# Half-height matmuls for the score tiles and dense blocks, columns loaded tile by tile, and the dots' small chain on GpSimd

## The chip, the cores and the metric

One Trainium2 chip, one of its cores. The metric is the device time of one execution in microseconds (us); before, the median of three runs was 1926.75 us (1924.97 to 1935.35).

Short names used below: PE is TensorE, PEld its weight loads, DVE VectorE, ACT ScalarE, POOL GpSimd, SP the SyncE queue that issues most DMAs.

## The reference

The layer takes x of 2048 tokens by 512 numbers, normalizes it and returns x + attention(xn) + experts(xn).

```
xn = layernorm(x)
# attention: 32 query heads of 16 numbers, one key/value head
scores = einsum("bhqd,bkd->bhqk", q, k) * (16 ** -0.5)
o = softmax(scores) @ v ; attention = o @ wo
# experts: 32 heads, 64 x 64 = 4096 experts addressed by two keys
s1 = einsum("nhd,ed->nhe", q1, k1) ; s2 = einsum("nhd,ed->nhe", q2, k2)
# the two best of each, their four sums, the two best of these: experts and gates
g = softmax(top_s) ; ue = u[top_e] ; ve = v[top_e]
act = gelu(einsum("nd,nhkd->nhk", xf, ue))
experts = einsum("nhk,nhk,nhkd->nd", g, act, ve)
```

## The kernel before

**Stages.** The tokens are four groups of 512 (GT = 4 tiles of 128 tokens). A short start normalizes, transposes x into `XT` (four tiles of 128 by 512 columns, each as a high and a low part) and projects q, k and v. Then 256 attention steps run, and everything else is put into the gaps of these steps.

**One attention step** (`att_steps`) issues on PE, in this order: four score matmuls (`sc`, two pairs; a pair is two matmuls of 64 rows each, one on the upper and one on the lower half of the array), eight `pv` matmuls in tiles of 32 columns, four more `sc`, and then the *fill*: whatever `run_scores` takes from the generator `score_thread`. ACT makes the exponentials (`pt`) of the four pairs. Between the `pv` and the second `sc` the function `mid` records the expert work: the tanh of a group of four gathered experts (`tanhs`), work of earlier steps put off in the lists `ON_ACT`, `LAST`, `LATER` and `BEHIND`, the dots of gathered rows with xn (`dots`), the weighted sums (`adds`), and new gathers. A fill ends when the cost counter `spent` (0.235 for one full matmul, `UNIT`) reaches the step's aim or has grown by 4.0 (`MOST`).

**What fills.** For each of 32 pairs (token group, chunk of heads) in `SEQ`, `item` makes four score tiles `psc`: 12 matmuls of 128 rows by 512 columns, whose result DVE reads with eight MAX8 and eight FIND_INDEX8. After the fourth tile `batch` turns these into gates and indices on DVE and POOL. For token groups 0 and 1 the experts are gathered row by row with indirect DMAs on the POOL queue (512 gathers, 128 groups of four). For groups 2 and 3 `dense` goes through all experts instead: 32 blocks, each with a `pact` tile (12 matmuls, then ACT Square and two DVE reads, later tanh and a split into `wd`), and for each pair of blocks four `pout` tiles (`sums`: six matmuls each and one DVE add). Before the blocks a stage of `pg` matmuls spreads the gates. `block_out` makes the attention's output (`pwo`).

**Buffers.** All of `psc`, `pact`, `pout`, `pwo`, `pg`, `pw` share three PSUM buffers:

```
xtile = lambda name: ps.tile([P, 512], F32, name=name, tag="x", bufs=3)
```

A new tile takes the buffer that was given back first; its first matmul waits for the last reader of the tile that held it.

**Order.** Inside the 256 steps the order on each engine is the order of recording; nothing is rescheduled. Every engine works through its list in order, so a wait holds up all that stands behind it on that engine.

**The dots' chain.** After the fourth dot of a group, three small DVE operations of 128 by 4 (`CHAIN`, L997 to L999) prepare the gelu; ACT does the tanh (L1004) in the next step; a fourth small DVE operation (`weigh`, L1011) makes the weights w of the four sums (L1023).

**Columns.** `load_phase2_xt` loads the next token group's columns into a new set of `XT` tiles (four DMAs of 512 KB) in the last tile of the old group, and `score_thread` ends that fill early.

Of the kernel before, what the change touches and what calls it, by code (L numbers as in the profile page):

```python
# [55 lines left out]
def tile_kernel(ctx, tc, x, wq, wkv, wo, wqT, kT, uv, ub, vb, out):  # L56
# [70 lines left out]
    XT, XN, ACC, XP = {}, {}, {}, [None]  # L127
# [65 lines left out]
    def project_kv(g):  # L193
        p = stile("pkv")[:, 0, :]
        n = 0
        for k in range(KC):
            for a, b in TERMS:
                w = (wkv_h, wkv_l)[a]
                nc.tensor.matmul(p[:32, :], w[:, k, :], XT[g][k][:, b, :], start=n == 0, stop=n == 11)
                n += 1  # L200
# [20 lines left out]
    def project_q(g, wqs):  # L221
        pq = xtile("pqs")
        for r in range(KC):
            p = stile("pq")[:, 0, :]
            n = 0
            for k in range(KC):
                for a, b in TERMS:
                    nc.tensor.matmul(p, wqs[k][:, a, r * P:(r + 1) * P], XT[g][k][:, b, :],
# [282 lines left out]

    def item(n_, ti, make=()):
# [5 lines left out]
        if jb == 0:  # L518
            m8 = small.tile([P, BT, 8, 8], F32, name="m8", bufs=1)
            i8 = small.tile([P, BT, 8, 8], U32, name="i8", bufs=1)  # L520
            M8[ph, c, b], I8[ph, c, b] = m8, i8
        m8, i8 = M8[ph, c, b], I8[ph, c, b]
        p = xtile("psc")

        last = ti == TPH - 1
        more = nc_ is not None and not (ph >= NSP and c == NC - 1)
        read = more and n_ + 1 >= NC
        n = 0
        for k in range(KC):
            for a, bb in TERMS:  # L530
                nc.tensor.matmul(p, XT[g][k][:, a, j * P:(j + 1) * P], WC[n_][k][:, bb, :],  # L531
                                 start=n == 0, stop=n == 11)
                n += 1
            if read and ti == 0 and k < 2:
                wp_read(n_ + 1, range(2 * k, 2 * k + 2))
            if last and more and nph != ph:
                load_phase2_xt(nph, k)
# [5 lines left out]
        for s in range(8):  # L543
            nc.vector.max(m8[:, jb, s, :], p[:, s * E:(s + 1) * E])  # L544
        for s in range(8):
            nc.vector.max_index(i8[:, jb, s, :], m8[:, jb, s, :], p[:, s * E:(s + 1) * E])  # L546
        if jb == BT - 1:
            batch(ph, c, b)
# [107 lines left out]
    def dense(DG, after):  # L656
# [72 lines left out]
        def activations(b, us, p):  # L729
            n = 0  # L730
            for k in range(KC):
                for a, c in TERMS:
                    nc.tensor.matmul(p, us[:, a, k * P:(k + 1) * P], XT[DG][k][:, c, :],  # L733
                                     start=n == 0, stop=n == 11)
                    n += 1
                yield k

        def first(b):
            p = xtile("pact")
            for k in activations(b, early[b], p):  # L740
                if k < KC - 1:
                    yield 3 * UNIT
            g, y = gate_rows(b), hh[:, b, :]
            nc.scalar.activation(y, p, AF.Square, scale=C_CUB ** 0.5)
            nc.scalar.copy(g, p)
            nc.vector.scalar_tensor_tensor(y, y, C_IN, p, op0=OP.add, op1=OP.mult)

            def go():
                nc.scalar.activation(y, y, AF.Tanh)
                behind(lambda: nc.vector.scalar_tensor_tensor(y, y, 1.0, g, op0=OP.add, op1=OP.mult))  # L750

            LATER.append(go)
            yield 3 * UNIT
# [11 lines left out]
        yield from first(0)  # L765
        rest_of_first = first(1)
        yield from islice(rest_of_first, 2)
# [37 lines left out]
        yield from rest_of_first  # L805
# [43 lines left out]
        held, ready, used = [], [], [0]  # L849

        def sums():

            used[0] += 2
            if formed[0] < used[0]:
                flush()
            for j in range(GT):
                p = xtile("pout")
                n = 0
                for wd, vs in ready:
                    for a, c in TERMS:  # L860
                        nc.tensor.matmul(p, wd[0][:, a, j * P:(j + 1) * P], vs[:, c, :], start=n == 0, stop=n == 5)  # L861
                        n += 1
                acc = ACC[GT * DG + j]
                nc.vector.tensor_add(acc, acc, p)  # L864
                yield 6 * UNIT

        stt = nc.vector.scalar_tensor_tensor
        for b in range(NB):
            wd = []
            if b > 1:  # L870
# [5 lines left out]
                p = xtile("pact")  # L876
                for k in activations(b, splits[b][0], p):
                    if k == 0:
                        store(lambda b=b: fetch_gates(b + 1))
                        if b % 2 == 0 and b > 2:  # L880
                            later_split(b + 2)
                        if b == 2:

                            store(load_totals)
                    if k == KC - 1 and b == NB - 1 and after is not None:
                        wp_read(after, range(2))
                    if b == NB - 1 and after is not None:
                        load_phase2_xt(SEQ[after][0], k)
                    if k < KC - 1:
                        yield 3 * UNIT  # L890

                if b not in fetched:
                    if b > 3 and formed[0] < b - 2:
                        flush()
                    run(STORES)
                    assert b in fetched
            vs = splits.pop(b)[1]
            gy = gates[b]
            if b > 2:
                gates.pop(b - 1)  # L900
            g, y = (gy[:, 0, :], gy[:, 1, :]) if b > 1 else (gy[:, b, :], hh[:, b, :])

            def gated(g=g, p=None):
                stt(g, g, 1.0 / GS, p, op0=OP.mult, op1=OP.mult)

            def whole(y=y, g=g):
                stt(y, y, 1.0, g, op0=OP.add, op1=OP.mult)

            def scaled(y=y, g=g):
                multiplied[0] += 1  # L910
                stt(g, g, 1.0 / GS, y, op0=OP.mult, op1=OP.mult)

            def high(y=y if b > 1 else g, wd=wd):
                wd.append(late[0].tile([P, 2, 512], F32R, name="wd", tag="wd", bufs=4))
                nc.scalar.copy(wd[0][:, 0, :], y)
                behind(lambda: low(y, wd[0]))

            def low(y, wd):
                nc.vector.tensor_tensor(out=wd[:, 1, :], in0=y, in1=wd[:, 0, :], op=OP.subtract)  # L919
                formed[0] += 1  # L920

            if b > 1:
                nc.scalar.activation(y, p, AF.Square, scale=C_CUB ** 0.5)
                stt(y, y, C_IN, p, op0=OP.add, op1=OP.mult)
                LAST.append(lambda y=y: nc.scalar.activation(y, y, AF.Tanh))
                if b == 3:

                    behind(lambda gated=gated, g=g, p=p: gated(g, p))
                else:
                    gated(g, p)  # L930
                behind(whole)
                LATER_ACT.append(high)
            else:
                LATER.append(lambda scaled=scaled, high=high: (behind(scaled), on_act(high)))
            held.append((wd, vs))
            if b > 1:
                yield 3 * UNIT
# [4 lines left out]
            for _ in range(b - 1 if b in (2, 3) else 0):  # L942
                if out_ready():
                    block_out()
                    yield 3.6
            if b % 2:
                if b > 1:
                    later_split(b + 2)
# [6 lines left out]
        yield from sums()  # L955
        if after is not None:
            wp_read(after, range(2, KC))
        OUTS.extend(range(GT * DG, GT * DG + GT))
# [8 lines left out]
    CHAIN = []  # L967
# [13 lines left out]
    def dot(m):  # L981
# [8 lines left out]
        if i == SB - 1:  # L990
# [5 lines left out]
            stt = nc.vector.scalar_tensor_tensor  # L996
            CHAIN.append(lambda: stt(q, a, C_CUB, a, op0=OP.mult, op1=OP.mult))  # L997
            CHAIN.append(lambda: stt(y, q, C_IN, a, op0=OP.add, op1=OP.mult))
            CHAIN.append(lambda: nc.vector.tensor_tensor(out=pairs(ga), in0=pairs(a), in1=gg, op=OP.mult))  # L999
            TH[n], GA[n] = y, ga  # L1000

    def tanh(n):
        th = small.tile([P, SB], F32, name="gth", bufs=3)
        nc.scalar.activation(th, TH[n], AF.Tanh)  # L1004
        TH[n] = th

# [365 lines left out]
```

## Time and profile before

| | |
|---|---|
| median of three runs | 1926.75 us |
| the profiled execution | 1925.78 us, its span 1924.1 us |
| PE busy | 1863.8 us (97%) |
| DVE busy | 1634.0 us (85%) |
| ACT busy | 1294.2 us (67%) |
| POOL busy | 700.8 us (36%) |
| `psc`, `pact`, `pout` on PE | 1536, 768 and 768 matmuls |
| DMA | 255 GB/s on average |

Busy time is the union of an engine's instructions. Matmuls overlap each other, so a start-to-start distance tells more than a duration. The span goes from the first to the last instruction; 1.7 us of the execution lie around it.

### The profile page before, as it was taken

The numbers are of one execution on the slowest core, as the hardware profiler recorded it, in microseconds if no ns is written. First come the engines' busy times: TensorE is split into PE (matmuls) and PEld (weight loads), VectorE is DVE, ScalarE is ACT, GpSimd is POOL, SyncE is SP. The second block draws the span as 40 slices with busy tenths as digits, with TensorE's granted clock in tenths as the row PEclk, the third lists the DMA queues.
The fourth block names the chain that finished last, engine by engine and source line by source line (L and its number), as shares of the span: only waits on it lengthen the run. The fifth ranks groups of instructions, "written<-read, shape, count | busy, mean of one in ns | idle before, by whom it ended". The sixth has DMA issues, their size and how long they took to land.

```text
span 1924.1 us, 34929 instructions
## 1 busy us (share of the span) xinstructions
PE 1863.8 (97%) x10990; PEld 991.8 (52%) x10990; DVE 1634.0 (85%) x6381; ACT 1294.2 (67%) x1803; POOL 700.8 (36%) x920
## 2 busy tenths in 40 slices
PE   6979999999999999999999999999999999999998
PEld 3634444555555554555555554555555455555553
DVE  6627787989998977999999897899988779999994
ACT  3346666655557887787877555555578777888873
POOL 1203334434452223343444444355422134344430
PEclk9989999999999899999999999999988899999999
DMA  7857789787773778888999987876736778899882
GB/s 274 315 186 278 266 272 301 279 296 251 249 246 122 233 240 249 253 288 270 287 300 309 362 287 237 280 256 220 242 105 220 249 215 292 271 284 286 282 277 84
DMA packets 234395, 491.13 MB, mean 255 GB/s; under 512 B 93396, under 2 KB 93396, under 8 KB 234204
## 3 DMA queue, kind: packets, MB, share of 16 engines
q0 software_dynamic: 73728, 268.47, 42.0%
q1 hardware_dynamic: 159240, 219.56, 34.9%
q8 instruction: 88, 1.44, 0.3%
q10 hardware_dynamic: 1236, 0.82, 0.1%
q14 instruction: 103, 0.84, 0.1%
HBM read 427.41 MB, written 56.07 MB: 251 GB/s over the span
## 4 chain that ended last, share of the span: by engine, by line
PE 85%; DMA 3%; ACT 3%; DVE 1%; issue 1%; SPq 0%; DVEq 0%; ACTq 0%
PE pv L340 24%; PE psc L531 18%; PE sc L326 17%; PE pact L733 9%; PE pout L861 9%; PE pg L815 3%; PE pwo L433 2%; ACT pt L329 2%; PE pw L486 1%; DMA wqt<-in_wqT_dram 1%; DMA dinv<-rc 1%; DMA wk<-dw 1%; PE pwt L493 0%; PE pwl L408 0%; DMA qa<-dqh 0%
## 5 line engine op out<-in xcount | busy, mean ns | idle before, releaser
L329 ACT ACTIVATE pt<-sc 128x1024 f32<-128x1024 f32 x1024 | 993.7, 1026 | 461.9 <-PE sc L326 460.5
L976 POOL DMA_INDIRECT g<-in_uv_dram,idx x512 | 556.8, 1087 | 1002.0 <-DVE xa L1023 531.0
L340 PE MATMUL pv<-pt,vaug 128*32 128x512 f32 x4096 | 516.4, 623 | 0.0
L531 PE MATMUL psc<-wk,xt 128*128 128x512 f32 x1536 | 388.7, 401 | 4.1 <-DVE wk L496 3.5
L326 PE MATMUL sc<-qa,kaug 64*128 64x512 f32 x2048 | 384.2, 451 | 8.6 <-ACT pt L329 8.4
L1023 DVE SCALAR_TENSOR_TENSOR xa<-g,w,xa 128x512 f32<-128x512 f32 x512 | 371.7, 744 | 0.1
L988 DVE CUSTOM_DVE_ANT_0 g<-g,xa 128x512 f32<-128x512 f32 x512 | 335.5, 681 | 7.4 <-DMA g<-in_uv_dram,idx 7.4
L531 PEld LDWEIGHTS psc<-wk,xt 128*128 128x128 f32 x1536 | 277.9, 188 | 107.7 <-issue 37.5
L326 PEld LDWEIGHTS sc<-qa,kaug 64*128 64x128 f32 x2048 | 155.9, 185 | 329.3 <-ACT pt L329 218.8
L340 PEld LDWEIGHTS pv<-pt,vaug 128*32 128x32 f32 x4096 | 109.6, 111 | 257.0 <-issue 255.4
L546 DVE FIND_INDEX8 i<-m,psc 128x8 uint32<-128x64 f32 x1024 | 206.3, 220 | 0.0
L733 PE MATMUL pact<-xt,wk 128*128 128x512 f32 x768 | 195.9, 400 | 0.0
L861 PE MATMUL pout<-wk,wd 128*128 128x512 f32 x768 | 194.8, 401 | 0.2 <-DVE wd L919 0.2
L544 DVE MAX8 m<-psc 128x8 f32<-128x64 f32 x1024 | 146.2, 213 | 41.1 <-PE psc L531 40.3
L861 PEld LDWEIGHTS pout<-wk,wd 128*128 128x128 f32 x768 | 140.8, 188 | 47.3 <-DVE act L988 5.5
L733 PEld LDWEIGHTS pact<-xt,wk 128*128 128x128 f32 x768 | 139.4, 188 | 48.5 <-issue 17.5
L698 DVE TENSOR_TENSOR wk<-rw,wk 128x512 fp32r<-128x512 f32 x128 | 84.8, 683 | 9.7 <-ACT wk L697 9.7
L864 DVE TENSOR_TENSOR da<-da,pout 128x512 f32<-128x512 f32 x128 | 82.8, 679 | 10.1 <-PE pout L861 10.0
L783 DVE TENSOR_TENSOR oh<-oh 128x2048 f16<-128x2048 f16 x64 | 78.0, 1219 | 0.8 <-ACT oh L759 0.6
L815 PEld LDWEIGHTS <-oh 128*128 128x128 f16 x1024 | 68.4, 162 | 13.8 <-issue 6.4
L1011 DVE SCALAR_TENSOR_TENSOR w<-gth,ga 128x4 f32<-128x4 f32 x128 | 20.4, 159 | 64.5 <-ACT gth L1004 64.0
L815 PE MATMUL pg<-oh 128*128 128x32 f16 x1024 | 73.5, 247 | 0.6 <-DVE oh L786 0.5
(159 smaller groups left out, 1411.1 us busy)
## 6 DMA issues: line engine op xcount, KB each, us to landing
wk<-dw SPq DMA_DIRECT2D x96, 512.0 KB
wqt<-in_wqT_dram SPq DMA_DIRECT2D x32, 512.0 KB
dw<-wk SPq DMA_DIRECT2D x32, 512.0 KB
rw<-in_ub_dram SPq DMA_DIRECT2D x64, 256.0 KB
rw<-in_vb_dram SPq DMA_DIRECT2D x64, 256.0 KB
gy<-dg SPq DMA_DIRECT2D x64, 256.0 KB
qa<-dqh SPq DMA_DIRECT2D x128, 64.0 KB
g<-in_uv_dram,idx POOLq DMA_INDIRECT x512, 6.0
```

What stands on the lines that cost most here:

```text
L326: nc.tensor.matmul(p[:, b, :], kaug[o:o + 64, kc * P:(kc + 1) * P], QA[u][o:o + 64, i, :], start=True, stop=True)
L329: nc.scalar.activation(pt, p, AF.Exp, scale=SCALE)
L340: nc.tensor.matmul(PV[u][32 * j:32 * j + 32, :], vaug[:, kc, :], pt[:, b, :], start=kc == 0, stop=kc == 15)
L531: nc.tensor.matmul(p, XT[g][k][:, a, j * P:(j + 1) * P], WC[n_][k][:, bb, :], start=n == 0, stop=n == 11)
L544: nc.vector.max(m8[:, jb, s, :], p[:, s * E:(s + 1) * E])
L546: nc.vector.max_index(i8[:, jb, s, :], m8[:, jb, s, :], p[:, s * E:(s + 1) * E])
L733: nc.tensor.matmul(p, us[:, a, k * P:(k + 1) * P], XT[DG][k][:, c, :], start=n == 0, stop=n == 11)
L815: nc.tensor.matmul(p[:, i * NB:(i + 1) * NB], oa[:, :, i], ob[:, :, i], start=True, stop=True)
L861: nc.tensor.matmul(p, wd[0][:, a, j * P:(j + 1) * P], vs[:, c, :], start=n == 0, stop=n == 5)
L976: nc.gpsimd.indirect_dma_start(out=gt, out_offset=None, in_=uv, in_offset=bass.IndirectOffsetOnAxis(ap=IDX[ph, c, ti][:, s:s + 1], axis=0))
L988: nc.vector.tensor_tensor_reduce(u, u, XN[TPH * ph + ti], scale=1.0, scalar=0.0, op0=OP.mult, op1=OP.add, accum_out=a[:, i:i + 1])
L1023: nc.vector.scalar_tensor_tensor(acc, v, w[:, i:i + 1], acc, op0=OP.mult, op1=OP.add)
```

## The change

**Half products.** From the last chunk of token group 0 on (`n_ >= NC - 1`), and in the dense blocks, `item`, `first`, `dense` and `sums` no longer issue matmuls; they yield objects `Tile` that hold the 12 or 6 operand pairs and a function `done` for what reads the result. `run_scores` collects the tiles of one fill and hands them to `products`. Of these, the last ones with up to 12 matmuls together are done *half*: each matmul of 128 rows becomes two of 64 rows. The upper halves (rows 0 to 63) are issued in this fill, alternating with the lower halves (rows 64 to 127) of the tiles kept from the fill before (`HALF`), whose `done` follows. Other tiles of the fill are done whole, after that. Where the upper list has 12 and the lower 6 (or the other way round), the six left over are issued alone.

**Columns tile by tile.** There is one set of `XT` tiles. `load_xt` loads 128 of the 512 columns (four DMAs of 128 KB) after the last use of these columns, in `done` of each tile; the early end of the fill is gone.

**Chain on GpSimd.** The chain is recorded at once after the fourth dot as four POOL operations, and the weights are two POOL operations recorded with the tanh; `CHAIN` and `weigh` are gone.

```diff
+    def products(tiles):
+        n, first = 0, []
+        while tiles and not tiles[-1].alone and n + len(tiles[-1].steps) <= 12:
+            n += len(tiles[-1].steps)
+            first.insert(0, tiles.pop())
+        a = [(t, i, 0) for t in first for i in range(len(t.steps))]
+        b = [(t, i, 1) for t in HALF for i in range(len(t.steps))]
+        if first or any(t.alone and t.steps for t in tiles):
+            for i in range(max(len(a), len(b))):
+                for run_ in (a, b):
+                    if i < len(run_):
+                        t, k, half = run_[i]
+                        t.mm(k, half)
+            for t in HALF:
+                t.done(t.p)
+            HALF[:] = first
+        for t in tiles:
+            t.whole()
...
+        def mm(self, i, half=None):
...
+                o = slice(64 * half, 64 * half + 64)
+                nc.tensor.matmul(self.p, w[o], v[o], start=i == 0 and half == 0, stop=i == n - 1 and half == 1)
...
+        tile_ = Tile("psc", steps, done)
+        if n_ >= NC - 1:
+            yield tile_
+            return
...
-            if b % 2:
-                if b > 1:
-                    later_split(b + 2)
-                if ready:
-                    for _ in range(2):
-                        if formed[0] < used[0] + 2:
-                            yield None
-                    yield from sums()
-                ready, held = held, []
+            if b % 2 == 0 and b > 3:
+                yield from ready(b - 4)
+                yield from sums(b - 4, (2, 3))
+            if b % 2 and b > 1:
+                yield from ready(b - 3)
+                yield from sums(b - 3, (0, 1))
...
-            stt = nc.vector.scalar_tensor_tensor
-            CHAIN.append(lambda: stt(q, a, C_CUB, a, op0=OP.mult, op1=OP.mult))
-            CHAIN.append(lambda: stt(y, q, C_IN, a, op0=OP.add, op1=OP.mult))
-            CHAIN.append(lambda: nc.vector.tensor_tensor(out=pairs(ga), in0=pairs(a), in1=gg, op=OP.mult))
+            V = nc.gpsimd
+            V.tensor_mul(q, a, a)
+            V.tensor_scalar(q, q, C_CUB, C_IN, op0=OP.mult, op1=OP.add)
+            V.tensor_mul(y, q, a)
+            V.tensor_tensor(out=pairs(ga), in0=pairs(a), in1=gg, op=OP.mult)
...
     def tanh(n):
         th = small.tile([P, SB], F32, name="gth", bufs=3)
-        nc.scalar.activation(th, TH[n], AF.Tanh)
-        TH[n] = th
+        nc.scalar.activation(th, TH.pop(n), AF.Tanh)
+        ga = GA.pop(n)
+        w = small.tile([P, SB], F32, name="w", bufs=3)
+        nc.gpsimd.tensor_mul(w, th, ga)
+        nc.gpsimd.tensor_add(w, w, ga)
+        WT[n] = w
...
-    def load_phase2_xt(g, k):
-        if k == 0:
-            XT[g] = []
-        xt = big.tile([P, 2, 512], F32R, name="xt", tag="xt", bufs=4)
-        nc.sync.dma_start(raw(xt[:]), d_xt[g - 1][k])
-        XT[g].append(xt)
+    def load_xt(g, j=None):
+        c = slice(0, 512) if j is None else slice(j * P, (j + 1) * P)
+        for k in range(KC):
+            nc.sync.dma_start(raw(XT[k][:, :, c]), d_xt[g - 1][k][:, :, c])
```

More of the change, by code (lines that the diff above doesn't have):

```diff
@@ L510, in tile_kernel, with __init__, whole @@
     BT = 4
+    class Tile:
+        def __init__(self, name, steps, done, alone=False):
+            self.name, self.steps, self.done, self.alone, self.p = name, steps, done, alone, None
+        def mm(self, i, half=None):
+            if self.p is None:
+                self.p = xtile(self.name)
+            w, v = self.steps[i]
+            n = len(self.steps)
+            if half is None:
+                nc.tensor.matmul(self.p, w, v, start=i == 0, stop=i == n - 1)
+            else:
+                o = slice(64 * half, 64 * half + 64)
+                nc.tensor.matmul(self.p, w[o], v[o], start=i == 0 and half == 0, stop=i == n - 1 and half == 1)
+        def whole(self):
+            for i in range(len(self.steps)):
+                self.mm(i)
+            self.done(self.p)
+    class Plain:
+        alone, steps = True, ()
+        def __init__(self, fn):
+            self.whole = fn
+    HALF = []
+    def products(tiles):
[16 more added lines that the diff above has]
+            t.whole()
     def item(n_, ti, make=()):
@@ L517, in item, with done @@
         b, jb = divmod(ti, BT)
[L518 to L525, printed above, removed]
         more = nc_ is not None and not (ph >= NSP and c == NC - 1)
         read = more and n_ + 1 >= NC
-        n = 0
-        for k in range(KC):
[L530 to L537, printed above, removed]
+        steps = [(XT[k][:, a, j * P:(j + 1) * P], WC[n_][k][:, bb, :]) for k in range(KC) for a, bb in TERMS]
+        def done(p):
+            if read and ti == 0:
+                wp_read(n_ + 1)
+            if more and nph != ph:
+                load_xt(nph, j)
+            if jb == 0:
+                M8[ph, c, b] = small.tile([P, BT, 8, 8], F32, name="m8", bufs=1)
+                I8[ph, c, b] = small.tile([P, BT, 8, 8], U32, name="i8", bufs=1)
+            m8, i8 = M8[ph, c, b], I8[ph, c, b]
+            for s in range(8):
+                nc.vector.max(m8[:, jb, s, :], p[:, s * E:(s + 1) * E])
+            for s in range(8):
+                nc.vector.max_index(i8[:, jb, s, :], m8[:, jb, s, :], p[:, s * E:(s + 1) * E])
+            if jb == BT - 1:
+                batch(ph, c, b)
+        tile_ = Tile("psc", steps, done)
+        if n_ >= NC - 1:
+            yield tile_
+            return
+        for k in range(KC):
+            for i in range(3 * k, 3 * k + 3):
+                tile_.mm(i)
             if k < KC - 1:
@@ L542, in item @@
                 yield from islice(make, 1)
[L543 to L548, printed above, removed]
+        done(tile_.p)
         yield 3 * UNIT
@@ L848, in dense, with sums, done, ready @@
             yield 2.0
[L849 to L854, printed above, removed]
-                flush()
[L856 to L865, printed above, removed]
+        held, used = {}, [0]
+        def sums(b, js, last=None):
+            for j in js:
+                steps = [(held[b + i][0][0][:, a, j * P:(j + 1) * P], held[b + i][1][:, c, :])
+                         for i in range(2) for a, c in TERMS]
+                def done(p, j=j):
+                    acc = ACC[GT * DG + j]
+                    nc.vector.tensor_add(acc, acc, p)
+                    if j == js[-1] and last is not None:
+                        last()
+                yield Tile("pout", steps, done, last is not None and after is None)
+        def ready(b):
+            for _ in range(3):
+                if formed[0] < b + 2:
+                    yield None
+            if formed[0] < b + 2:
+                flush()
         stt = nc.vector.scalar_tensor_tensor
@@ L892, in dense @@
[L892 to L920, printed above, removed]
@@ L1290, in mid @@
                     sums = 0
[L1291 to L1292 removed]
                 def go():
                     n = sums
[L1296 removed]
+                    while rest or n > 0:
                         if n > 0:
```

170 lines of the change are left out of this document (83 added, 87 removed).

## The prediction

> **What bounds the kernel now.** I read the page's busy times, then its chain of waits by engine, then the busy times of three stages that the change touches: score tiles, first dense stage, score tiles again.
>
> ```profile
> PE 1863.8 (97%) x10990; PEld 991.8 (52%) x10990; DVE 1634.0 (85%) x6381; ACT 1294.2 (67%) x1803; POOL 700.8 (36%) x920
> ...
> PE 85%; DMA 3%; ACT 3%; DVE 1%; issue 1%; SPq 0%; DVEq 0%; ACTq 0%
> ...
> 353.00:597.00 244.00, 242.39 (x1384) 134.24 (x1380) 225.44 (x1446) 142.31 (x175) 116.38 (x214) 1.00 0.74 258
> 752.00:1073.00 321.00, 320.39 (x1816) 176.12 (x1812) 299.18 (x702) 251.87 (x357) 131.21 (x116) 1.00 0.90 285
> 1073.00:1398.00 325.00, 324.14 (x1821) 174.65 (x1814) 294.22 (x1814) 189.14 (x231) 151.64 (x249) 1.00 0.78 265
> ```
>
> The columns of a stage are its length, then PE, PEld, DVE, ACT and POOL busy. PE hardly idles (242.39 of 244), the chain is PE's, and DVE stands right behind at 91 to 93%. So PE time saved counts until it meets DVE, and DVE's lag decides the rest. One attention step on PE:
>
> ```profile
> 1206.59 0.50 PE L326 MATMUL sc<-qa,kaug 64*128 64x512 f32 x2
> 1206.93 0.40 PE L326 MATMUL sc<-qa,kaug 64*128 64x512 f32 x2
> 1207.26 0.50 PE L531 MATMUL psc<-wk,xt 128*128 128x512 f32 x1
> 1207.59 0.39 PE L531 MATMUL psc<-wk,xt 128*128 128x512 f32 x1
> ...
> 1210.56 0.39 PE L531 MATMUL psc<-wk,xt 128*128 128x512 f32 x1
> 1210.88 0.50 PE L326 MATMUL sc<-qa,kaug 64*128 64x512 f32 x2
> 1211.22 0.39 PE L326 MATMUL sc<-qa,kaug 64*128 64x512 f32 x2
> ```
>
> This fill has 15 matmuls; from the 2nd to the 15th are 13 distances in 2.97 us, 0.228 each. Four distances are longer: last `sc` pair to first `psc` 0.33, first to second `psc` 0.33, last `psc` to `sc` 0.32, first to second `sc` pair 0.34. Over 0.228 each, that is 1.32 - 0.91 = 0.41 us for going from the 64-row form to the 128-row form and back.
>
> **Half products: the form.** A fill of half products alone stays in the form of `sc`, and the 0.41 goes. In the order in which the changed kernel's instructions stand, 177 fills have half products; 99 have nothing else, 78 have whole tiles (or `pwo`, `pg`) beside them and change form as before. Gain 99 x 0.41 = 40.6 us.
>
> **Half products: the slots.** A slot is a pair of halves, upper and lower. No fill of before has more than two pairs in a row, so its steady price isn't shown. In the rows above a second `sc` pair follows the first after 0.34, a second `psc` its first after 0.33, and the next form follows after 0.33 and 0.32: pairs and whole matmuls agree wherever both can be compared. I take 0.228. Below one weight load, 0.19 in the next rows, I put no slot; the upper bound is 0.34, a pair's distance with its load exposed.
>
> ```profile
> 1206.59 0.19 PEld L326 LDWEIGHTS sc<-qa,kaug 64*128 64x128 f32 x2 [0.84 <-ACT pt L329]
> 1210.88 0.30 PEld L326 LDWEIGHTS sc<-qa,kaug 64*128 64x128 f32 x4 [0.35 <-issue]
> ```
>
> Four loads end within 0.30 us of the first: those of the second pair run while the first pair's matmuls (0.50 from 1210.88) are under way on the same rows. That is what makes 0.228 possible. [...]
>
> Slots cost where lists are unequal. The order holds 3900 halves, which stand for 1950 whole matmuls, in 177 x 12 = 2124 slots: in most dense fills a `pact` of 12 meets one `pout` of 6, and six slots use half the array. The excess is 174 slots x 0.228 = 39.7 us, nearly all in the two dense stages. Form and slots together: 39.7 - 40.6 = -0.9 us. The change gives back in the dense blocks what it gains on the score tiles.
>
> **New wait: three PSUM buffers.** A half tile keeps its buffer into the next fill. So in a fill that has upper halves, kept tiles and whole tiles, a whole tile can need the buffer of a tile that was finished only in this fill, and PE waits until it is read; the next step's `sc`, `pv` and so ACT's exponentials queue behind it. The order with its waits shows two patterns. (i) In 14 dense fills two kept `pout` tiles finish, and a whole `pact` waits for the add of the first. (ii) In 10 a kept `pact` finishes, two whole `pout` tiles follow, and the second waits for the two DVE reads of that `pact`. What such reads take now:
>
> ```profile
> 838.24 3.07 PE L861 MATMUL pout<-wk,wd 128*128 128x512 f32 x12
> 841.24 0.91 PE L326 MATMUL sc<-qa,kaug 64*128 64x512 f32 x4
> ...
> 838.42 0.15 DVE L1011 SCALAR_TENSOR_TENSOR w<-gth,ga 128x4 f32<-128x4 f32 x1
> 843.54 1.28 DVE L864 TENSOR_TENSOR da<-da,pout 128x512 f32<-128x512 f32 x2
> ...
> 872.64 2.34 PE L733 MATMUL pact<-xt,wk 128*128 128x512 f32 x9
> 875.36 0.61 ACT L923 ACTIVATE gy<-pact 128x512 f32<-128x512 f32 x1
> 877.17 0.67 DVE L924 SCALAR_TENSOR_TENSOR gy<-gy,pact 128x512 f32<-128x512 f32 x1
> 877.77 0.67 DVE L904 SCALAR_TENSOR_TENSOR gy<-gy,pact 128x512 f32<-128x512 f32 x1
> ```
>
> The fill of two `pout` tiles starts at 838.24, but DVE first works through the step's sums and put-off work behind w (838.42) and adds only at 843.54; the first tile is free at 843.54 + 1.28/2 = 844.18, 5.94 after the fill's start. In pattern (i) the whole `pact` is due 11 x 0.228 + 0.33 = 2.84 after it: 3.1 us of waiting if DVE lags as here, none if its queue were empty. I take 1.8, the upper part: the work ahead of the add is the step's own and can't start before w, though a longer step lets DVE catch up. 14 x 1.8 = 25 us (0 to 43). In (ii) the `pact` ends at 874.98 and is free at 878.44, 3.46 later; without a queue it is 0.61 + 2 x 0.67 = 1.95. The second `pout` is due 1.4 after that end (0.33 + 0.33 + 5 x 0.228 after the last slot's start, less its 0.39). Waits of 0.5 to 2.0; I take 1.0, 10 us (5 to 20). Two fills at the start of the dense blocks, where a whole `pout` waits for the one just before it: 1.5 each, 3 us (1 to 6). Sum 38 us (6 to 69).
>
> The score stages have more room. There a tile is read 5.7 us or more before its buffer is wanted (`sc`, `pv`, `sc` 3.0, and one tile 2.7), and DVE reads it in 2.7:
>
> ```profile
> 1210.36 1.14 DVE L544 MAX8 m<-psc 128x8 f32<-128x64 f32 x8
> L546 DVE FIND_INDEX8 i<-m,psc 128x8 uint32<-128x64 f32 x1024 | 206.3, 220 | 0.0
> ```
>
> That is 1.14 + 8 x 206.3/1024 = 2.75. PE waits only where DVE lags by over 3 us.
>
> **Chain on GpSimd.** DVE loses four operations per group, POOL gains six, 768 in all.
>
> ```profile
> L1011 DVE SCALAR_TENSOR_TENSOR w<-gth,ga 128x4 f32<-128x4 f32 x128 | 20.4, 159 | 64.5 <-ACT gth L1004 64.0
> L999 DVE TENSOR_TENSOR ga<-act,gg 128x4 f32<-128x4 f32 x128 | 20.2, 158 | 0.0
> L998 DVE SCALAR_TENSOR_TENSOR gy<-gq,act 128x4 f32<-128x4 f32 x128 | 20.2, 158 | 1.6
> L997 DVE SCALAR_TENSOR_TENSOR gq<-act 128x4 f32<-128x4 f32 x128 | 20.1, 157 | 0.4
> ...
> 1207.05 0.26 POOL L590 CAST fi<-i 128x64 f32<-128x64 uint32 x1 [4.72 <-DVE i L546]
> 1208.48 0.71 POOL L601 TENSOR_TENSOR e<-fi 128x16 f32<-128x16 f32 x1
> 1210.60 0.22 POOL L604 TENSOR_TENSOR e<-e,cond 128x16 f32<-128x16 f32 x1
> 1211.20 0.21 POOL L606 CAST idx<-fi 128x32 int32<-128x32 f32 x1
> ...
> 1208.37 2.07 DVE L1023 SCALAR_TENSOR_TENSOR xa<-g,w,xa 128x512 f32<-128x512 f32 x3
> ```
>
> DVE saves at most 81 us busy; PE being the bound, this buys nothing directly but pays for the waits below. A small POOL operation takes 0.71 while DVE does its sums and 0.22 while it reads PSUM, so 768 take 169 to 545 us, which POOL's 700.8 of 1924 leaves room for. The three sums of 2.07 take 0.69 each beside POOL's operations, so DVE isn't slowed by them. [...]
>
> The chain's cost is its place. On POOL the two operations for w stand behind the gathers and `batch` of the step before, and DVE's sums, its put-off work and the next tile's reads stand behind w. After a batch POOL is busy from 1207.05 to 1211.41; w would be there at 1211.41 + 2 x 0.22 = 1211.85, where the sums now start at 1208.37: 3.5 us late. 32 batches, and with 1.75 dots a step a group is weighed every 2.3 steps: 14 meetings, up to 49 us of DVE, against the 81 it is spared. Of this PE sees what exceeds the 3 us of room: 14 x 0.4 = 5 us (0 to 49).
>
> **Columns tile by tile.** 52 DMAs in place of 16 on SP's queue, the same bytes. Columns are wanted four tiles, three steps or some 20 us, after they were asked for; I take nothing. The empty fill at a change of groups goes too; I count no gain.
>
> **Sum.** The profiled execution took 1925.78, close to the median 1926.75. 1925.8 - 0.9 + 38 + 5 = 1968 us. With the bounds of the waits 1931 to 2043; the upper ends don't come together, so 1938 to 2005 is this case's own range.
>
> **The rivals.** Faster: slots at 0.21, between 0.19 and 0.228, give 2124 x 0.018 = 38 us, and DVE, relieved of 81 us, halves the dense waits (19 us): 1968 - 57 = 1911. For it, two loads side by side take no longer than one; against it, `sc` pairs show no sign of being quicker. Chance 0.17.
>
> Same: the buffers come back in time, because DVE's lag goes with the chain. 1968 - 43 = 1925. Against it, in the rows above the add stood behind 5 us of DVE work of which the chain is a few tenths. Chance 0.13.
>
> Slower, by GpSimd: if w is late after most batches and in the dense steps too, DVE becomes the bound of the score stages, and the full 49 us come: 1968 + 44 = 2012. It decides when DVE idles more than the 7 to 9% that it has. Chance 0.12.
>
> Slots with exposed loads (the load waits for the matmuls of its rows): 0.34 each, 2124 x 0.11 = 234, 2202 us. The load row speaks against it. Chance 0.03.
>
> **How the numbers follow.** My case has 0.55. A difference under 0.5% (10 us) can hardly be told from none here. Faster takes 0.17 from its rival; same 0.13; slower is the rest, 0.70. For 8 in 10 the range goes from 1905, a little under the faster rival's time, to 2012, GpSimd's.
>
> **What would show it.** Right: `psc` fills of 12 slots with 0.23 from pair to pair and steps of 5.7 us; dense stages longer by 30 to 60 us in sum, with PE idle before whole `pact` and `pout` tiles, released by the DVE add L904 and read L951; score stages shorter by some 20 us; small POOL operations at 0.2 to 0.7. Wrong: slots off 0.23 by over 0.01 (21 us), no idle time before those tiles, or DVE's sums waiting for POOL's w by over 50 us in all.

## The result, and the profile after

The changed kernel takes 2134.6 us (median of 4 runs, 2129.04 to 2148.36), the kernel before on the same chip 1925.95 us: 1.1087 times as long, 95% interval 1.1043 to 1.113. The forecast was 1968 us, 1905 to 2012. The direction was right, the size was not. The profiled execution's span is 2130.9 us, 206.8 more than before.

The page's busy times, and its chain of waits by engine:

```profile
PE 1955.4 (92%) x12940; PEld 1097.7 (52%) x12940; DVE 1599.9 (75%) x5869; ACT 1291.7 (61%) x1803; POOL 969.5 (45%) x1688
...
PE 61%; DVE 18%; ACT 6%; POOL 4%; issue 3%; DMA 2%; SPq 0%; ACTq 0%; POOLq 0%; DVEq 0%
```

PE is busy 91.6 us longer and yet a smaller share of the span (97% to 92%); DVE now has 18% of the chain where it had 1%. To find the place I cut both traces at the starts of the attention steps:

```
steps                      before     after   change (us)
28-62    score tiles        237.4     236.6     -0.8
62-87    totals, one-hots   153.9     160.7     +6.8
87-133   first dense loop   321.4     432.7   +111.3
133-150  score tiles        118.1     118.2     +0.1
150-182  score tiles        222.9     224.9     +2.0
182-205  totals, one-hots   152.2     142.9     -9.3
205-253  second dense loop  335.5     425.6    +90.1
```

All but a few us lie in the two loops of the dense blocks. Their busy times, first in the kernel before (columns: from and to, length, then busy PE, PEld, DVE, ACT, POOL, the granted clock PEclk, DMA share, GB/s):

```profile
737.30:1058.70 321.40, 320.79 (x1810) 175.45 (x1808) 297.52 (x692) 251.77 (x357) 132.64 (x119) 1.00 0.89 282
1551.80:1887.40 335.60, 335.31 (x1887) 182.49 (x1885) 312.03 (x732) 261.69 (x370) 133.73 (x118) 1.00 0.86 270
```

and in the changed one:

```profile
749.60:1182.30 432.70, 379.30 (x2282) 217.83 (x2283) 297.36 (x587) 252.40 (x360) 207.85 (x295) 0.88 0.67 213
1668.20:2093.80 425.60, 380.73 (x2358) 217.11 (x2356) 310.09 (x610) 262.18 (x373) 206.96 (x303) 0.92 0.68 214
```

PE idles 53.4 and 44.9 us where it idled 0.6 and 0.3: 97.4 us more. The granted clock was 1.00 and is 0.88 and 0.92; by the trace's clock records PE stood at half clock (0.5 in the records) for 101.4 and 64.9 us of the two loops. That loses at most half of it, 83 us, and 74 us if the 18 us are left out in which PE idled at half clock anyway. Idle time and clock are thus 171 to 181 of 201 us; 20 to 30 us are left for the slots (below). In the kernel before PE had next to no waits there; the only rows, first loop and second loop (us in total, times, longest), are

```profile
PE sc L326 <- ACT pt L329: 0.6, 2, 0.4
PE pout L861 <- DVE wd L919: 0.2, 1, 0.2
```

In the changed kernel, first loop and then second loop, the longest are

```profile
PE pact L528 <- DVE wk L753: 32.5, 11, 3.6
PE pact L525 <- DVE da L904: 8.8, 7, 1.7
PE pact L528 <- ACT wk L752: 5.8, 12, 1.2
PE pout L528 <- DVE da L904: 3.0, 1, 3.0
PE pout L525 <- DVE gy L951: 1.7, 4, 0.4
```

```profile
PE pact L528 <- DVE wk L753: 30.2, 11, 3.6
PE pact L528 <- ACT wk L752: 6.2, 11, 1.2
PE pact L525 <- DVE da L904: 4.7, 5, 2.4
PE pout L525 <- DVE gy L951: 1.7, 4, 0.4
```

The forecast waits are there (L904, L951), 20 us of them in these rows. The large one, 62.7 us for L753 and 12.0 for L752, was in no term of the prediction. These two lines are the *split*: a block's rows are cut into a high part by an ACT copy (L752) and a low part by a DVE subtraction (L753), and its first product `pact` reads both. One step of the first loop, by the timeline (start, length, in brackets the idle time before and what ended it):

```profile
822.90 1.14 ACT L752 CAST wk<-rw 128x512 fp32r<-128x512 f32 x2
823.57 0.50 PE L528 MATMUL pact<-xt,wk 64*128 64x512 f32 x1 [1.17 <-ACT wk L752]
...
824.60 0.69 DVE L954 SCALAR_TENSOR_TENSOR gy<-gy 128x512 f32<-128x512 f32 x1 [1.54 <-ACT gy L972]
825.21 0.74 DVE L1063 SCALAR_TENSOR_TENSOR xa<-g,w,xa 128x512 f32<-128x512 f32 x1
825.87 0.69 DVE L966 TENSOR_TENSOR wd<-gy,wd 128x512 fp32r<-128x512 f32 x1
826.47 0.75 DVE L1063 SCALAR_TENSOR_TENSOR xa<-g,w,xa 128x512 f32<-128x512 f32 x1
827.13 1.29 DVE L753 TENSOR_TENSOR wk<-rw,wk 128x512 fp32r<-128x512 f32 x2
827.88 0.79 PE L528 MATMUL pact<-xt,wk 64*128 64x512 f32 x1 [3.57 <-DVE wk L753]
...
829.75 2.76 PE L528 MATMUL pact<-xt,wk 64*128 64x512 f32 x6
832.43 2.89 PE L525 MATMUL pout<-wk,wd 128*128 128x512 f32 x6
835.26 0.73 PE L327 MATMUL sc<-qa,kaug 64*128 64x512 f32 x4
```

The fill starts with a half of `pact`; its split is being made in this very step, and on DVE it stands behind the sums and the put-off work (824.60 to 827.13). PE waits 1.17 and 3.57 us. Then, with everything at hand, six slots take 2.68 us and six whole `pout` matmuls 2.83, about twice 0.228 each: the clock stands at one half from 824.92 on for 10.24 us.

The diff has the reason: the split is asked for one block ahead (`later_split(b + 1)`) where it was two (`later_split(b + 2)`).

### The profile page after: what moved, and what is told of

It is laid out like the page before. It is cut to its first block, busy times and chain, and to the rows that moved or that the text cites. A ratio compares the mean times of both kernels' runs of the same rounds, so it can differ in the third digit from the quotient of the medians.

```text
span 2130.9 us, 39237 instructions
## 1 busy us (share of the span) xinstructions
PE 1955.4 (92%) x12940; PEld 1097.7 (52%) x12940; DVE 1599.9 (75%) x5869; ACT 1291.7 (61%) x1803; POOL 969.5 (45%) x1688
## 4 chain that ended last, share of the span: by engine, by line
PE 61%; DVE 18%; ACT 6%; POOL 4%; issue 3%; DMA 2%; SPq 0%; ACTq 0%; POOLq 0%; DVEq 0%
PE pv L341 16%; PE sc L327 11%; PE pact L528 9%; PE psc L528 5%; PE psc L525 5%; DVE xa L1063 5%; PE pout L525 4%; DVE i L587 4%; ACT pt L330 3%; PE pg L860 3%; PE pact L525 3%; DVE m L585 2%; PE pwo L434 2%; DVE g L1033 2%; PE pout L528 1%
## 5 line engine op out<-in xcount | busy, mean ns | idle before, releaser
L1063 DVE SCALAR_TENSOR_TENSOR xa<-g,w,xa 128x512 f32<-128x512 f32 x512 | 372.8, 748 | 86.3 <-POOL w L1054 84.7
L528 PE MATMUL pact<-xt,wk 64*128 64x512 f32 x1128 | 281.8, 450 | 76.6 <-DVE wk L753 64.6
L528 PEld LDWEIGHTS pact<-xt,wk 64*128 64x128 f32 x1128 | 200.4, 217 | 134.3 <-DVE wk L753 75.1
L528 PE MATMUL psc<-wk,xt 64*128 64x512 f32 x1896 | 240.0, 390 | 6.0 <-DVE i L587 4.6
L528 PEld LDWEIGHTS psc<-wk,xt 64*128 64x128 f32 x1896 | 191.6, 185 | 41.2 <-DVE i L587 7.3
L1042 POOL TENSOR_TENSOR gq<-act 128x4 f32<-128x4 f32 x128 | 62.3, 487 | 327.3 <-DVE act L1033 326.8
L528 PE MATMUL pout<-wk,wd 64*128 64x512 f32 x876 | 206.9, 409 | 3.8 <-DVE da L904 3.8
L1053 POOL TENSOR_TENSOR w<-gth,ga 128x4 f32<-128x4 f32 x128 | 45.4, 355 | 345.5 <-ACT gth L1050 330.5
L525 PE MATMUL psc<-wk,xt 128*128 128x512 f32 x588 | 157.7, 409 | 8.4 <-DVE i L587 4.9
L904 DVE TENSOR_TENSOR da<-da,pout 128x512 f32<-128x512 f32 x128 | 85.1, 684 | 105.6 <-PE pout L525 81.4
L528 PEld LDWEIGHTS pout<-wk,wd 64*128 64x128 f32 x876 | 144.8, 191 | 18.4 <-DVE da L904 4.7
L525 PEld LDWEIGHTS psc<-wk,xt 128*128 128x128 f32 x588 | 105.6, 190 | 57.4 <-issue 21.4
```

Source lines behind the costliest of these rows:

```text
L525: nc.tensor.matmul(self.p, w, v, start=i == 0, stop=i == n - 1)
L528: nc.tensor.matmul(self.p, w[o], v[o], start=i == 0 and half == 0, stop=i == n - 1 and half == 1)
L1063: nc.vector.scalar_tensor_tensor(acc, v, w[:, i:i + 1], acc, op0=OP.mult, op1=OP.add)
```

## The experiments

The first theory was that lead alone: a split made one block ahead makes PE wait, and the clock falls behind each wait. Rivals: the three PSUM buffers (1), the chain on GpSimd (2), the half form (3).

**The old kernel with the short lead.**

```diff
-                        if b % 2 == 0 and b > 2:
-                            later_split(b + 2)
+                        if b > 3:
+                            later_split(b + 1)
 ...
-                if b > 1:
-                    later_split(b + 2)
```

> The kernel before, of which only the weights' split of the dense blocks is put off: each block's rows are split in the step in which its first product is emitted (one block ahead, as in the changed kernel), no longer two blocks ahead. No half products, no chain on GpSimd. Theory (the split's lead is what cost the time, with the clock that falls after each wait): the two dense stages, 321.4 and 335.5 us before, become longer by 40 to 100 us each, TensorE idles before 'pact' for the split's DVE half, the granted clock in them leaves 1.00, and the time is 2010 to 2130 us. Rival 1 (three PSUM buffers and whole tiles that wait for the adds): nothing of it is in this kernel, 1926 us. Rival 2 (the dots' chain on GpSimd): 1926 us. Rival 3 (the half form itself): 1926 us.

Measured 1973.36 us, 1.0258 (1.0228 to 1.0289). Dense loops:

```profile
742.30:1088.00 345.70, 330.99 (x1810) 180.42 (x1808) 296.83 (x690) 251.17 (x357) 126.84 (x117) 0.97 0.83 260
1575.70:1933.50 357.80, 343.39 (x1884) 185.67 (x1882) 313.88 (x733) 261.01 (x370) 133.79 (x119) 0.98 0.81 253
```

The mechanism is there without half products (27.0 us of waits for the split's DVE half, 34.2 us at half clock) and costs 0.0258 x 1923.34 = 50 us, below the expected 84 to 204: a quarter of what was to be explained.

**The changed kernel with the long lead**, and a control for the buffers that this takes.

```diff
-NGB = 12
-NWK = 8
+NGB = 10
+NWK = 10
 ...
-                    later_split(b + 1)
+                    later_split(b + 2)
 ...
                 later_split(4)
+                later_split(5)
```

> The changed kernel, with the split two blocks ahead again. The buffers for that come from the gathers (10 row buffers for 12, and 10 weight buffers for 8). Half products, tile order and chain stay. Theory: the waits for the split (62.7 us for its DVE half in the two dense stages) all but go, the granted clock there is 0.97 or more, the two stages, 432.7 and 425.6 us, come to 330 to 365 us each, and the time is 1930 to 2000 us. Rival 1 (PSUM buffers): the waits for the adds stay and the time is over 2080 us. Rival 2 (chain on GpSimd): over 2080 us. Rival 3 (half form): over 2080 us.

> The changed kernel with 10 row buffers for the gathers instead of 12 and nothing else: what the buffers taken in the run with the split two blocks ahead cost by themselves. All theories: 2125 to 2165 us, the dense stages within 10 us of 432.7 and 425.6.

Measured 2115.58 us, 1.0981 (1.094 to 1.1021), and 2221.82 us for the control with `NGB = 10` alone (one run). The theory missed its range and the rivals' "over 2080" came true; the control missed too, as two row buffers fewer cost 87 us. In the control DVE's dots wait 109 us for gathered rows (8.6 in the changed kernel), and the split stands behind them. Against the control the long lead brings 106 us, but the comparison with the changed kernel itself is spoilt. The run does show one thing: the waits for the split fall to 1.1 us, and those for L904 and L951, the reads that rival 1 is about, come to 35.5 and 48.5 us in the two loops.

**Whole tiles in the dense blocks.**

```diff
-                yield Tile("pact", activations(us), done)
+                yield Tile("pact", activations(us), done, True)
```

and the same for `first` and `sums`.

> The changed kernel with the dense blocks' products as whole tiles, in the same steps and with the split one block ahead; score tiles stay halves. Theory (split's lead): TensorE still idles for the split in the dense stages, they stay 380 us or longer each, and the time is 2060 to 2150 us. Rival 1 (whole tiles that wait for a PSUM buffer that the kept half holds): the waits for the adds' buffers go, 2090 to 2120 us. Rival 3 (the half form itself): the dense stages are back at 320 to 345 us each, 1930 to 1960 us.

Measured 1973.98 us (one run), far below what the first theory gave and a little above rival 3's range. Dense loops:

```profile
747.40:1091.50 344.10, 326.86 (x1810) 176.54 (x1808) 291.56 (x581) 252.16 (x358) 206.38 (x291) 1.00 0.83 265
1584.30:1935.10 350.80, 339.10 (x1884) 182.09 (x1882) 304.91 (x607) 261.73 (x370) 213.78 (x303) 1.00 0.83 259
```

With the lead unchanged, 163 us (858.3 to 694.9) of the 201 are gone: 69 of idle time, 72 to 82 of lost clock, the others of the rest. So the theory fell in its first form, but the run can't tell the half form itself from what comes with it. The new theory: what costs is the *place in the fill*. `products` takes the last tile of a fill, which in these fills is mostly the newest `pact`, and puts a half of it first; as a whole tile it mostly stands behind a `pout` or two (18 of the 28 `pact` in the first loop of this run). The newest tile is the one whose weights are late.

**Whole `pout` tiles first, and the split early on DVE.**

```diff
+        ahead = [t for t in tiles if getattr(t, "name", "") == "pout"]
+        for t in ahead:
+            t.whole()
         if first or any(t.alone and t.steps for t in tiles):
```

```diff
-            behind(lambda: nc.vector.tensor_tensor(out=w[:, 1, :], in0=rw[:, i, :], in1=w[:, 0, :], op=OP.subtract))
+            sub = lambda: nc.vector.tensor_tensor(out=w[:, 1, :], in0=rw[:, i, :], in1=w[:, 0, :], op=OP.subtract)
+            sub() if b > 4 else behind(sub)
```

> The changed kernel, in which a fill of the dense blocks emits its whole 'pout' tiles ahead of the half pairs instead of behind them; same tiles per fill, same splits, same chain. The run with whole dense tiles (1974.0 us) has shown that the split one block ahead alone costs some 40 us, and that the half form adds some 160 in the dense stages, where the changed kernel puts the newest 'pact' first in the fill. Theory (place in the fill: the half of a 'pact' stands first, before its weights are split, each wait is followed by microseconds of half clock): the 74.7 us of waits for the split in the two stages come to less than 35 us, the time at half clock (167 us) to less than 60, the stages to 345 to 375 us each, 1970 to 2040 us. Rival 1 (whole tiles wait for the PSUM buffer of the kept half, the waits for the adds): these go too, as a whole tile now stands a step behind it, but they were 20 us of waits, so 2090 to 2115 us if only they counted. Rival 3 (the half form itself is slow in the dense stages, 64 rows of 'pact' and 'pout'): over 2100 us.

> The changed kernel, in which from block 5 on VectorE's half of the split stands at once behind ScalarE's copy, ahead of the dots, not among the adds behind them. Fill order, buffers and chain stay. Theory (place in the fill against the split): the waits for VectorE's split fall from 62.7 us in the dense stages to less than 20, 2000 to 2070 us; what stays is ScalarE's half (12 us) and the waits for the adds. Rival 1 (PSUM buffers): the waits for the adds stay and the time stays over 2100 us. Rival 3 (half form): over 2100 us.

> The changed kernel with both: whole 'pout' tiles ahead of the half pairs, and VectorE's half of the split ahead of the dots. Each alone left 71 and 76 us of idle TensorE in the dense stages (the changed kernel 98, the kernel before 1). Theory (split and PSUM waits add up and take each other's place): idle falls to 25 to 50 us, time at half clock to under 30 us, the dense stages to 345 to 375 us each, 2000 to 2050 us. Rival (the half form itself costs the rest in these stages): idle falls as said, but the stages stay at 385 us or more, 2060 us or more.

Measured 2085.05 us (1.0832, 1.0805 to 1.086), 2070.65 us (1.0779, 1.0746 to 1.0811) and, both together, 2084.8 us (1.0826, 1.0785 to 1.0867). The first is just below rival 1's range, the second at the upper edge of the theory's, the third above the theory's and in its rival's, though idle time didn't fall as that rival said. The early split takes the largest wait away (L753 to 0.5 us in both loops), and in its place come the forecast ones. Its waits in the second loop:

```profile
PE pout L528 <- DVE gy L952: 10.2, 8, 1.7
PE pact L525 <- DVE da L905: 9.0, 5, 5.0
PE pout L525 <- DVE gy L952: 7.8, 5, 2.0
PE pact L528 <- ACT wk L752: 6.2, 11, 1.2
```

L905 and L952 are L904 and L951 of the changed kernel, the reads that give PSUM buffers back. In both loops they come to some 61 us, three times what they were while PE waited for the split. With both edits the half of `pact` itself waits for the add of the whole `pout` that now precedes it. First loop of that run:

```profile
PE pact L525 <- DVE da L909: 16.1, 7, 2.4
PE pact L528 <- DVE da L909: 14.5, 5, 3.3
```

So the two causes don't add up, they stand behind each other: 87 us of idle time stayed where 25 to 50 were expected. The loops of this run are 147 us longer than before; beside the idle time at most 35 are lost clock (69 us at half clock), and 26 or more are left for the slots, so the half form itself is a small part. Three buffers with one kept from fill to fill look like a bound of their own, as rival 1 had it. That is read from what released the waits; no run changed the number of buffers.

**Work in the waits.** Eight spare products ahead of the half pairs:

```diff
+            if first and first[0].name == "pact" and len(first[0].steps) and dense_on[0] == 1:
+                t = first[0]
+                t.p = xtile(t.name)
+                for i in range(8):
+                    nc.tensor.matmul(t.p, XT[0][0:64, 0, 0:P], XT[0][0:64, 0, :], start=True, stop=True)
```

> The changed kernel, with 8 spare half products (64 rows, ready operands, into the PSUM tile that the first real product then clears) ahead of the half pairs of each fill of the dense blocks that starts a 'pact': 40 fills, 8 x 0.228 = 1.8 us of work each, 73 us of work in all. It takes no wait away and only keeps TensorE busy where it waits. Theory (idle of over some 1.5 us in a window of 3.41 us brings half clock, and that costs 167 us at half clock, 84 us): in the 23 fills with waits the spare products are hidden in the wait, in the other 17 they cost 31 us, the time at half clock falls from 167 us to less than 60, and the time is 2050 to 2110 us although work was added. Rival (the low clock stands beside waiting and costs nothing by itself): 2150 to 2210 us.

Measured 2139.19 us (1.1109, 1.1065 to 1.1153), between the two expectations. Dense loops:

```profile
747.20:1174.00 426.80, 394.42 (x2438) 234.88 (x2436) 297.04 (x586) 252.31 (x360) 208.26 (x295) 0.94 0.68 215
1662.30:2097.60 435.30, 410.22 (x2518) 241.43 (x2516) 310.88 (x611) 262.17 (x373) 206.79 (x303) 0.94 0.67 210
```

The loops take 862.1 us for 858.3, with 73 us of work added. Idle time fell by 41 us and half clock from 166 to 109, at most 29 us of loss: 73 - 41 - 29 = 3, and 3.8 were measured. So the low clock does cost time by itself; the waits that stayed kept it low more often than I expected (under 60).

**The rest of the 38 us with whole tiles.** The early split, on top of whole dense tiles:

> The changed kernel with whole tiles in the dense blocks (1974.0 us, dense stages 344.1 and 350.9) and VectorE's half of the split ahead of the dots from block 5 on. Theory (the dense stages are 38 us longer than before with whole tiles because the split is made one block ahead): its waits go, the stages come to 322 to 332 and 336 to 346 us, 1940 to 1960 us, of which the chain on GpSimd is some 20. Rival (another part of the changed order of the dense blocks holds the 38 us): the stages stay at 340 or more, 1965 to 1985 us.

```profile
756.10:1085.30 329.20, 322.54 (x1810) 176.40 (x1808) 284.37 (x567) 252.55 (x358) 208.69 (x287) 1.00 0.84 267
1584.20:1925.60 341.40, 336.55 (x1885) 182.91 (x1884) 303.48 (x608) 262.04 (x370) 217.59 (x301) 1.00 0.84 265
```

The loops are where the theory put them, 13.6 us above before, of which 10.6 are idle time, nearly all waits for ACT's exponentials. The whole, 1963.48 us (1.0203, 1.0166 to 1.0241), is 3 us above its range: 24 us came off the loops in the profile, but a step behind the first loop took 18.1 us where it took 7.6 in the run without the early split. A single `pout` waits in it for the low part of `wd`, and 10.24 us at half clock go with it:

```profile
1095.83 0.79 PE L525 MATMUL pout<-wk,wd 128*128 128x512 f32 x1 [6.55 <-DVE wd L967]
```

**The chain.** Back on DVE in the changed kernel, and alone in the kernel before:

```diff
-            V = nc.gpsimd
-            V.tensor_mul(q, a, a)
+            CHAIN.append(lambda: stt(q, a, C_CUB, a, op0=OP.mult, op1=OP.mult))
 ...
```

> The changed kernel with the dots' chain back on VectorE as before; the rest stays. Theory (split and fill order in the dense stages): within 2% of the changed kernel, VectorE has some 35 us more in all to do and no longer waits 84.7 us for w, 2115 to 2150 us. Rival 2 (the waits for GpSimd's w delay the adds and the split behind them): 2000 to 2090 us.

> The kernel before with nothing but the dots' chain moved to GpSimd. Prediction's step: VectorE is relieved by up to 81 us and waits for w, 5 us for TensorE (0 to 49): 1915 to 1975 us. Theory (the chain is not what cost the time): 1915 to 1945 us. Rival 2 (the chain costs tens of us): over 1960 us.

Measured 2113.37 us (1.0996, 1.0966 to 1.1026) and 1943.97 us (1.0131, 1.0085 to 1.0177). The first is just under its range, the second at the upper end of the theory's. The chain on GpSimd costs some 20 us in either kernel, and next to nothing in the dense loops (322.6 and 335.3 us with it alone). In the kernel before, 8 of the 15 us by which the profiled execution got longer lie right behind the first loop, where `pout` waits 5.8 us for `wd` (L919), and 10.24 us at half clock go with it. With the chain on DVE the two long score stages take 229.1 and 216.4 us, 8.3 and 6.5 less than before; on GpSimd that gain was lost.

**Half products for the score tiles alone**, with the columns tile by tile, the dense blocks' loop as before and the chain on DVE; then with the last expert group before each dense stage as whole tiles:

```diff
-        tile_ = Tile("psc", steps, done)
+        tile_ = Tile("psc", steps, done, ph >= NSP and c == NC - 1)
```

> Half products for the score tiles alone, with the columns loaded tile by tile: the dense blocks' loop and its order are those of the kernel before, and the dots' chain is on VectorE. What the runs so far say: dense stages 321 and 336 us as before, the two long score stages some 15 us shorter as in the changed kernel with its chain on VectorE (229.1 and 216.4 us for 237.4 and 222.9), 4 us longer where the half pairs begin. Theory: 1900 to 1920 us, faster than both. Rival (the gain in the score stages comes back as a wait for VectorE's maxima or at the end): 1922 to 1940 us.

> As the run with half products for the score tiles alone and the chain on VectorE (1943.75 us), but the last expert group's tiles ahead of each dense stage are whole, so that no half is kept where the dense blocks begin. In that run the two long score stages were 6.7 and 9.4 us shorter than in the kernel before, and the stretches in which the dense blocks' gates are spread 10, 6, 5 and 5 us longer. Theory (the kept half delays the totals of the gates there): these come back, 1905 to 1925 us. Rival (their length has another cause, or is the spread of one profiled execution): 1930 to 1945 us.

Measured 1943.75 us (1.0089, 1.0056 to 1.0123), the rival and a little more. The second is 1927.37 us, between its two ranges, 1.0007 (0.9986 to 1.0028), no difference from the kernel before. The score stages gain 5.3 and 5.5 us in it, and behind the first dense loop one step of 16.6 us takes them back. The wait in it:

```profile
PE psc L528 <- DMA wk<-dw: 6.8, 2, 5.9
```

One wait of 5.9 us for the next chunk's weights, and 13.65 us at half clock that begin in it. Whether it comes in every execution wasn't tried. No version here is faster than the kernel before.

## Why the prediction was wrong

**Form and slots** (-0.9 us): right to within some 15 us. A score fill of half products in the changed kernel:

```profile
1306.64 3.04 PE L528 MATMUL psc<-wk,xt 64*128 64x512 f32 x24
1309.50 0.65 PE L327 MATMUL sc<-qa,kaug 64*128 64x512 f32 x4
1310.08 1.92 PE L341 MATMUL pv<-pt,vaug 128*32 128x512 f32 x16
```

Twelve slots and the way into `sc` take 2.86 us, 0.238 each with the passage counted; the rival with exposed loads at 0.34 is refuted. In the two long score stages 47 fills of halves alone should gain 47 x 0.41 = 19.3 and six more slots cost 1.4; of these 17.9 us 14.8 came with the chain on DVE. In the dense loops the trace has 144 slots more, at 0.228 each 32.8 us, and 40 fills of halves alone, which spare 16.4: +16.4 us, where the loops have 20 to 30 beside idle time and clock. The slots are near where the prediction put them.

**Three PSUM buffers** (38 us, 6 to 69): right in kind. Here they were 13.5 us in pattern (i), 3.4 in (ii) and 4.6 of other `pout` waits; once the wait ahead of them was gone they were 61. A wait's price depends on what is late before it.

**The list of new waits** is the step that failed. "The order with its waits shows two patterns", said the prediction. The same order had a third, the half of `pact` behind L752 and L753 of its own step; the prediction names neither the split nor its shorter lead. Together with the place of that half at the head of the fill it made 74.7 us of waits, where the sum had nothing. The prediction's own rule, to ask for each wait what DVE works through before, would have priced it: what stands ahead of the split from 824.60 to 827.13 is the kind of queue that the prediction had read between 838.42 and 843.54.

**The clock** is the second step that is missing. Every wait was priced at its length. The 97 us of idle time brought 74 to 83 more, not far from as much again.

**Chain on GpSimd** (5 us, 0 to 49): in range, but mis-sized; some 20 us. (14 x 0.4 is 5.6, a slip of no weight.)

```profile
L1063 DVE SCALAR_TENSOR_TENSOR xa<-g,w,xa 128x512 f32<-128x512 f32 x512 | 372.8, 748 | 86.3 <-POOL w L1054 84.7
...
L1042 POOL TENSOR_TENSOR gq<-act 128x4 f32<-128x4 f32 x128 | 62.3, 487 | 327.3 <-DVE act L1033 326.8
...
L1053 POOL TENSOR_TENSOR w<-gth,ga 128x4 f32<-128x4 f32 x128 | 45.4, 355 | 345.5 <-ACT gth L1050 330.5 <-ACT ex L638 14.5
```

The small operations take 0.31 to 0.49 us on average, inside 0.2 to 0.7. But DVE waits 84.7 us for w, over the 50 that the prediction named as a sign of being wrong: not 14 meetings with a batch but 58 waits, 24 of them in the dense loops. DVE's sums themselves stay at 748 ns (744 before); the 146 of them that start while one of these small operations runs take 749 ns on average, the 332 that meet none 748. POOL's operations are the ones that get longer: 155 of them start inside one of DVE's sums, and every one ends 0.05 to 0.06 us after that sum does. They take 0.62 us on average, against 0.20 with DVE idle.

**Columns tile by tile** (nothing): no wait for them appears among those of the loops or of the score stages.

## What to carry to other kernels

When a loop is re-ordered, list for each product how many steps lie between the making of its operands and its place, before and after; a producer that moves from "a step ago" to "this step" puts the whole queue of its engine in front of the consumer (here 2.5 us of DVE's work, 824.60 to 827.13, and a wait of 3.57). Don't put the newest tile at the head of a fill. Price a wait of a busy TensorE not at its length alone but with the clock behind it: in the changed kernel each us of waiting cost 0.8 to 0.9 us more, with the early split at most 0.3 (42 us at half clock for 76 of idle time), so it matters how the waits lie. And where one wait is removed, look for the next in line before counting the gain.

## What the runs showed of the clock

By the clock records the clock goes from 1.0 to 0.5 and back, and only on a grid of 3.413 us that runs through each trace. I took all windows of this grid at full clock in the dense loops of the fifteen traces and summed PE's idle time in each. With less than 1.0 us of it none was followed by half clock (2,733 windows), with 1.0 to 1.9 us 52 of 166 were, with more than 1.9 us all 118. In the changed kernel's trace alone these are none of 167, 9 of 17 and all 17. Half clock then lasted mostly one to three windows (up to six in two runs), sometimes through windows without any idle time; in the changed kernel's two loops it was 11 times one, 7 times two and 8 times three. All this is of the dense loops: elsewhere in the traces of the changed kernel and the one before, 23 windows with less than 1.0 us of idle time were followed by half clock.
